# An S4 convolution beside a GEGLU FFN: products by half, a pairs contraction, port-spread rows, and four U spectra chunks in the phase buffers

## The chip, the cores and the metric

The kernel runs on one core of one Trainium2 chip. The engines named here are PE (matrix products; PEld is its weight load), DVE, ACT and POOL (elementwise work) and SP, which in this kernel only issues DMAs. The metric is the device time of one execution in microseconds, lower is better; the value before is the median of three runs.

## The reference

The function mixes two branches of one input u [1, 2048, 640] in bf16:

```python
x = A_u
g = _sigmoid((x * gate_w).sum(-1, keepdims=True))
a = _A_ref(x, ...)       # S4
b = _B_ref(x, ...)       # (gelu(x @ w_gate) * (x @ w_up)) @ w_down, 640 -> 1728 -> 640
return g * a + (1 - g) * b
```

```python
logdA = dt * A                      # [D=640, N=128], complex
dB = dt * Bc
P = jnp.exp(logdA[:, :, None] * l[None, None, :])
K = jnp.einsum("dn,dnl,dn->dl", Cc, P, dB).real
...
Yf = Uf * Kf[None, :, :, :]         # FFT of length 4096 of u and of K, both padded with zeros
y = irfft(Yf)[..., :L]  +  u * Dskip
```

So per channel a kernel K of 2048 steps is generated from 128 complex modes, and u is convolved with it causally by a transform of length 4096.

## The kernel before, in words

One tile `arena` [128 partitions, 211,968 bytes] holds everything; regions are addressed by byte offsets (`O_XT` to `O_UA`, L254 to L268) and shared by names that live at different times. `Plan` records each step with what it reads, writes and overlaps (L77 to L120); `emit` (L128) replays a written-out list `ORDER` (L27 to L74): each number gives step, engine and PSUM bank pair. The order of instructions on each engine is thus fixed, and every DMA is issued from the SP queue in that order. The time estimates that `add` takes (first argument) belong to the planner and change nothing on the chip unless `ORDER` does.

The work, in the order in which it mostly runs:

- **FFN.** The 2048 rows go in two groups. For each of 14 column tiles of 128 of the 1728 columns, `gate` (L500, 10 matmuls of 512 columns) with the gelu on ACT (L504), `up` (L520) with the product on DVE (L524). `downs` (L540): 8 steps per group, each 28 matmuls (L548), evicted scaled by 1 - g (L245 on ACT, L249 on DVE). Plain evictions from PSUM are L243 (ACT) and L247 (DVE).
- **K generation**, `kgen(q)`, for each half q of the channels (W = 320 each). cs1 and cs2 hold two grids of complex exponentials, with four channels side by side (`quads`): `exps1` (L599, 32 exponentials of 320 elements on ACT), `phases` (L580, L582, L584 on DVE, the sine L589 on ACT), `grid1` (L613 twice and L614 once per group of rows), `neg1` (L619), `exps2` (L627, then L631 on DVE), `grid2` (L637).
- **Contraction**, `contract` (L650): 80 groups of four channels, two matmuls each with 128 weight columns (32 rows x 4 channels) and 80 moving columns (20 x 4); of the 4 x 4 channel pairs in the result only the diagonal is wanted. Seven evictions to kst; `pick` (L661) selects the wanted quarter with the matrix sel, and dS (DRAM) takes the half of K by four writes (L678). The first row of K comes apart (L669, L672, L676).
- **U transform**: L719, evictions, 16 writes of dU (L724).
- **Gathers** (L744, L752): 18 DMAs per half read dS into Kl, 128 partitions x 16 phases x 320; partition ranges 0:16, 16:32, 32:64, 64:128 come from different rows of dS.
- **Stage A** (L780) transforms Kl; eight writes per half into columns W*h of one DRAM tensor dKA (L784).
- **Stage B** (L807): the second step of the transform, in eight chunks of 4 of the 32 DRAM row groups, loaded by `loadB` (L794), for U (from dU) and for K (from dKA, both halves of the channels, hence after both stage A). `swap` (L820): two DMAs inside the arena that give a copy of the U spectrum with neighbouring partitions exchanged.
- **`mix`**, one per chunk: stage B of K, two products on DVE over all 640 channels (L826, L827, 2560 elements each), the inverse step (L834, four PSUM steps), one write of dY (L840).
- **`finish`**: eight loads of dY (L847), each of which needs rows of all eight chunks, through a ring of four tiles; the last matmuls (L854), the additions of the FFN part (L859), and 16 output writes (L863).

All U chunks of the spectra lie in the region of cs1 and cs2, so none is loaded before the second contraction has read it.

Of the kernel before, what the change touches and what calls it, by code (L numbers as in the profile page):

```python
# [27 lines left out]
    336 1392 652 276 12 296 356 436 616 476 636 948 516 24 376 416 316 456 496 964 556 536 44 596 1468 576 224 676  # L28
    696 64 896 936 856 2740 1448 876 396 984 6316 796 1484 816 916 836 1408 716 736 1544 2981 2836 776 756 1064 1428
    2862 3076 1004 1024 1044 4383 2956 2768 1124 1084 1104 2888 10580 10604 3008 4404 2782 10636 1508 3020 2804 2856  # L30
    1568 1604 2903 3096 248 3044 88 3101 2976 4428 1664 2602 1148 6320 3196 6348 2624 2924 1168 6362 2656 3220 6436
    6388 1524 1188 6416 3128 3463 3316 3248 4444 3142 1584 3556 3488 1628 3261 3216 3164 1204 6440 1688 3336 6483
    3822 3284 6556 6464 6508 1644 3501 1228 3916 6536 3848 3340 3576 1244 1264 4183 1284 3368 3436 3524 1704 6562
    4208 4276 6600 3581 6676 6588 6628 6656 3703 1724 3608 3676 1304 3622 3728 3796 3940 3696 1324 3644 1348 4061
    4036 104 3968 6683 1364 4156 6722 1944 6796 4088 3860 6748 2004 6708 1748 6776 3981 3936 3884 3382 4056 1828
    1764 4004 1788 4223 3456 3404 1868 1804 4300 4296 1908 1844 4244 128 1924 3741 4376 1884 1968 144 6802 3816 6843
    6916 3764 6828 1984 6868 168 6896 4101 2064 2028 4176 4328 6922 2124 6963 7036 6988 6948 4344 2088 7016 184 4124
    2044 7043 208 7082 7068 4460 2184 7156 7108 2148 7136 2104 2164 2208 9464 7161 7203 4488 4742 7276 7188 2224
    7228 7256 9524 2480 4768 2321 2504 2443 2344 2242 2464 2360 2264 2281 2384 2403 2304 7322 2424 9728 7280 4661
    7396 7304 7344 9768 9744 7376 9808 2523 9784 2560 4684 4502 2588 2544 9848 9824 2716 2736 9408 2696 9864 2676  # L40
    7401 4524 7440 4703 7516 7424 9888 7464 8276 8296 8236 9448 9904 7496 8316 8436 8336 4542 4724 8456 8536 8576
    9388 8416 8356 8396 8496 8476 8556 7521 4564 7560 9428 8256 4583 7636 7584 8376 8516 7544 7616 9488 4622 4604
    9548 9584 7680 7641 4648 9504 4783 7756 7668 7708 7736 4902 4808 4876 9644 5021 9608 4996 9564 7760 5116 7803
    7876 7824 7788 9668 9924 5260 7856 5048 4823 5356 9984 4928 7921 4896 7948 4844 7882 7996 7908 4941 5288 9684
    7976 5142 5016 4964 10008 8003 5236 8040 9624 5061 8116 8068 5136 10104 8028 5300 9948 8096 5383 5376 5324 5168
    10044 8160 5476 5408 8122 8188 5503 5084 8148 8216 9964 5420 5528 5596 9704 10068 5742 10024 5496 5444 8621
    10128 5836 8583 10164 5180 8608 11176 11356 8648 5623 10144 5256 5768 8676 5204 5861 5716 5648 10084 10188 5782
    5956 5540 5804 5856 5888 11536 10204 8723 5616 8682 5564 8708 10221 8748 10262 8776 10244 10300 10284 10343
    10324 10381 10364 8822 10404 8780 8848 10423 8808 10462 8876 10444 11221 11260 10488 11244 11183 11288 11302
# [91 lines left out]
def kernel(  # L141
# [90 lines left out]
    def evac(n, p, dst, src, r=(), w=(), rank=3.0, act=True, dve=True, scale=None, **k):  # L232
        e = {}
        if act:
            e["ACT"] = an(n)
# [21 lines left out]
    O_WD = O_ZA + 10240  # L257
    O_W = O_WD + 17920
    O_TB = O_W + 7680
    O_WA = O_TB + 384  # L260
    O_A = O_WA + 8192
    O_CS1 = O_A + 11520
    O_CS2 = O_CS1 + 40960
# [302 lines left out]
    def quads(ap):  # L566
        return ap.rearrange("p (k j) -> p k j", j=4)
# [390 lines left out]
```

## Time and profile before

| | us |
|---|---|
| median of three runs (326.82, 326.91, 329.02) | 326.91 |
| profiled execution | 327.61 |
| its span | 325.8 |
| mean granted PE clock | 0.922 |

| engine | busy us (share of the span) |
|---|---|
| PE | 266.1 (82%) |
| DVE | 246.3 (76%) |
| ACT | 223.6 (69%) |
| POOL | 5.3 (2%) |

Times within the profile are counted from the start of the span. In the first 30 us PE is busy 20.18, DVE 19.82 and ACT 25.18 us. The 40 slices of the span (busy tenths; PEclk is the granted clock in tenths) show where no engine is full:

```profile
PE   0799999897796999979899987985998889993452
...
DVE  4687999999999963799996977254363899982464
ACT  4998997699995599998989576525471386671000
...
PEclk9989999999797999999999997999899799998555
DMA  6993344332321144433437659979366569934997
```

One slice is 8.1 us. The first contraction lies at 100.4 to 107.8 us (slices 13 and 14 from the left), the second at 182.3 to 194.3, the gathers of the second half after it, and the loads of dY in the last four slices. Mean durations of DMAs from issue to landing, as far as the change touches them: dU write (320 KB) 2.3 us, dU load (640 KB) 4.7, dKA write (320 KB) 4.2, dKA load (640 KB) 6.0, swap (320 KB) 4.3, dY write (640 KB) 6.1, dY load (640 KB) 5.6, output (160 KB) 4.7 (medians).

### The profile page before, as it was taken

How to read it: one execution, taken by the hardware profiler on the slowest of the kernel's cores; microseconds unless marked ns; L12 is line 12 of the kernel's file. 1: busy time of each engine (PE TensorE's matmuls, PEld its weight loads, DVE VectorE, ACT ScalarE, POOL GpSimd, SP SyncE). 2: the span in 40 equal slices, each digit the busy share in tenths (PEclk: the TensorE clock that was granted, in tenths of full speed). 3: DMA queues.
4: the chain of work that ended last, by engine and by line, in shares of the span. 5: the costliest groups of instructions: out<-in, count | busy, mean ns of one | idle time of the engine just before them, and what ended most of it. 6: DMA issues, size and time to landing. Idle time of an engine off the chain costs nothing.

```text
span 325.8 us, 5490 instructions
## 1 busy us (share of the span) xinstructions
PE 266.1 (82%) x2112; PEld 146.7 (45%) x2126; DVE 246.3 (76%) x332; ACT 223.6 (69%) x307; POOL 5.3 (2%) x18
## 2 busy tenths in 40 slices
PE   0799999897796999979899987985998889993452
PEld 0254444443366677534344743432465456551220
DVE  4687999999999963799996977254363899982464
ACT  4998997699995599998989576525471386671000
POOL 3000000000000000000000000000110000000000
PEclk9989999999797999999999997999899799998555
DMA  6993344332321144433437659979366569934997
GB/s 171 394 331 104 121 140 125 100 103 81 125 76 42 62 123 130 143 123 120 141 100 240 188 192 291 341 163 260 115 204 221 181 240 330 344 141 163 368 353 245
DMA packets 47519, 60.57 MB, mean 186 GB/s; under 512 B 4419, under 2 KB 41862, under 8 KB 47494
## 3 DMA queue, kind: packets, MB, share of 16 engines
q1 hardware_dynamic: 47494, 60.23, 57.3%
q8 instruction: 16, 0.26, 0.3%
q14 instruction: 9, 0.07, 0.1%
HBM read 35.80 MB, written 19.17 MB: 169 GB/s over the span
## 4 chain that ended last, share of the span: by engine, by line
PE 36%; ACT 22%; DVE 18%; DMA 15%; issue 5%; SPq 3%; DVEq 0%; ACTq 0%
PE ps L548 13%; PE ps L520 8%; PE ps L500 7%; ACT arena L243 6%; ACT arena L589 5%; DVE arena L247 5%; DMA dKA<-arena 4%; ACT arena L599 4%; DMA arena<-dY 3%; DMA arena<-dU 3%; ACT arena L504 3%; DMA arena<-dKA 2%; DVE arena L859 2%; PE ps L650 2%; PE ps L807 2%
## 5 line engine op out<-in xcount | busy, mean ns | idle before, releaser
L243 ACT CAST arena<-ps 128x640 bf16<-128x640 f32 x111 | 70.6, 702 | 38.1 <-PE ps L807 15.7
L500 PE MATMUL ps<-arena 128*128 128x512 bf16 x276 | 66.5, 392 | 13.0 <-DMA arena<-in_u_T_dram 9.2
L247 DVE CAST arena<-ps 128x640 bf16<-128x640 f32 (+2 forms) x67 | 56.2, 881 | 20.1 <-PE ps L807 10.4
L520 PE MATMUL ps<-arena 128*128 128x512 bf16 x250 | 63.1, 401 | 4.2 <-DVE arena L524 1.9
L548 PE MATMUL ps<-arena 128*128 128x320 bf16 x448 | 65.0, 305 | 1.0 <-DVE arena L247 0.5
L548 PEld LDWEIGHTS <-arena 128*128 128x128 bf16 x448 | 44.5, 100 | 20.6 <-issue 2.1
L500 PEld LDWEIGHTS <-arena 128*128 128x128 bf16 x280 | 28.0, 100 | 47.9 <-issue 14.1
L520 PEld LDWEIGHTS <-arena 128*128 128x128 bf16 x260 | 26.5, 103 | 37.2 <-issue 9.3
L589 ACT ACTIVATE arena<-arena 128x2560 bf16<-128x2560 int16 x18 | 41.6, 2334 | 0.4 <-DVE arena L637 0.3
L524 DVE TENSOR_TENSOR arena<-ps,arena 128x1024 bf16<-128x1024 f32 x26 | 31.6, 1218 | 13.1 <-PE ps L520 12.9
L504 ACT ACTIVATE arena<-ps 128x1024 bf16<-128x1024 f32 (+1 forms) x28 | 27.7, 1023 | 9.4 <-PE ps L500 9.2
L807 PE MATMUL ps<-arena 64*64 64x320 bf16 x256 | 16.9, 325 | 9.0 <-DMA arena<-dKA 2.8
L599 ACT ACTIVATE arena<-arena 128x320 bf16<-128x320 f32 x64 | 23.3, 455 | 1.0 <-DVE arena L451 1.0
L854 PE MATMUL ps<-arena 128*64 128x320 bf16 x64 | 10.2, 474 | 14.5 <-DMA arena<-dY 14.5
L859 DVE SCALAR_TENSOR_TENSOR arena<-ps,g_f,arena 128x640 bf16<-128x640 f32 x16 | 13.0, 878 | 11.9 <-PE ps L854 11.9
L249 DVE TENSOR_SCALAR arena<-ps,omg 128x640 bf16<-128x640 f32 x10 | 8.8, 883 | 14.9 <-PE ps L548 14.9
L627 ACT ACTIVATE arena<-arena 128x320 bf16<-128x320 f32 x40 | 14.8, 455 | 5.9 <-PE ps L650 5.9
L582 DVE SCALAR_TENSOR_TENSOR arena<-arena 128x320 int32<-128x320 f32 x40 | 16.9, 483 | 0.8 <-ACT arena L589 0.7
L650 PE MATMUL ps<-arena 128*128 128x80 bf16 x320 | 13.5, 212 | 3.8 <-DVE arena L637 2.8
L807 PEld LDWEIGHTS <-arena 64*64 64x64 bf16 x256 | 8.2, 107 | 17.7 <-issue 9.7
L650 PEld LDWEIGHTS <-arena 128*128 128x128 bf16 x320 | 13.3, 107 | 4.6 <-DVE arena L637 3.5
L780 PE MATMUL ps<-arena 128*128 128x320 bf16 x64 | 12.1, 308 | 4.1 <-DMA arena<-dS 2.3
(93 smaller groups left out, 240.8 us busy)
## 6 DMA issues: line engine op xcount, KB each, us to landing
arena<-in_w_gu_dram SPq DMA_DIRECT2D x52, 160.0 KB, 2.2
dU<-arena SPq DMA_DIRECT2D x16, 320.0 KB, 2.3
arena<-dU SPq DMA_DIRECT2D x8, 640.0 KB, 4.7
dKA<-arena SPq DMA_DIRECT2D x16, 320.0 KB, 4.2
arena<-arena SPq DMA_DIRECT2D x16, 320.0 KB, 4.3
arena<-dKA SPq DMA_DIRECT2D x8, 640.0 KB, 6.0
dY<-arena SPq DMA_DIRECT2D x8, 640.0 KB, 6.1
arena<-dY SPq DMA_DIRECT2D x8, 640.0 KB, 5.6
```

Source lines behind the costliest of these rows:

```text
L243: nc.scalar.copy(out=dst, in_=src(b))
L247: nc.vector.tensor_copy(out=dst, in_=src(b))
L500: nc.tensor.matmul(ps[:, k + j, :], lhsT=Wg[w][:, kt, :], rhs=xT[2 * grp + j][:, kt, :], start=(kt == 0), stop=(kt == NKT - 1))
L504: add({"ACT": an(1024)}, lambda s: nc.scalar.activation(out=HTall[0:p, :, f, :], in_=ps[0:p, plan.bank(g):plan.bank(g) + 2, :], func=ACT.G ...
L520: nc.tensor.matmul(ps[:, k + j, :], lhsT=Wu[w][:, kt, :], rhs=xT[2 * grp + j][:, kt, :], start=(kt == 0), stop=(kt == NKT - 1))
L524: add({"DVE": v1(1024)}, lambda s: nc.vector.tensor_tensor(out=HTall[:, :, f, :], in0=ps[:, plan.bank(u):plan.bank(u) + 2, :], in1=HTall[: ...
L548: nc.tensor.matmul(ps[:, k + h, 0:W], lhsT=HTq[q][:, f, 128 * j:128 * j + 128], rhs=Wd[f][:, W * h:W * h + W], start=(f == 0), stop=(f == ...
L589: ac(an(8 * W), lambda: nc.scalar.activation(out=t[:], in_=ph.bitcast(I16)[:, :, :, 0:32:2], func=ACT.Sin, scale=SIN_SCALE), r=[f"ph{k}"], ...
L599: nc.scalar.activation(out=cs1[:, 1, :, 4 * s:4 * s + 4], in_=quads(aT[:, ds]), func=ACT.Exp, scale=float(sg * (4 + 8 * i)))
L650: nc.tensor.matmul(ps[:, k + i // g, 80 * (i % g):80 * (i % g) + 80], lhsT=cs1[:, x, k0 + i, :], rhs=cs2[:, x, k0 + i, :], start=(x == 0), ...
L807: nc.tensor.matmul(ps[64 * y:64 * y + 64, k + x, 0:W], lhsT=TB[64 * x:64 * x + 64, 0, :], rhs=t[64 * x:64 * x + 64, 2 * a + y, HV[h]], sta ...
L859: add({"DVE": v1(D)}, lambda s, p=p, ph=ph, z=z: nc.vector.scalar_tensor_tensor(out=z, in0=ps[:, plan.bank(p):plan.bank(p) + 2, 0:W], scal ...
```

## The change

1. **Products by half.** dKA becomes two DRAM tensors, one per half, so that a write is contiguous over 2560 bytes and a load has 320 KB. `mix` is split into `product(h, ...)` and `inverse`; a half's products need that half's stage A alone, and an inverse step of half h that half's products alone. dY becomes three tensors of 64, 32 and 32 rows (chunks 0 to 3, 4 and 5, 6 and 7), read back by 24 loads into eight tiles that are all resident.
2. **Pairs contraction.** Two channels lie side by side instead of four; 160 pairs, as two column halves (y) of PE, 320 matmuls per half with 64 weight columns and 40 moving columns; four evictions instead of seven. `exps1` writes a row and its mirror with one instruction of 640 elements, by way of a negated copy aN of aT. The first row of K is computed before `kgen(0)`.
3. **Port-spread rows.** The partitions of the transform are permuted: rows 0:16, 16:32, 32:64, 64:128 of the gathers go to partitions with strides 8, 8, 4 and 2. The rows of u_nat are permuted in the host's layout, and the tables' row numbers follow (`rows`, `last_rows`, five more fields). A fourth matrix is added to TB; nothing uses it, as SWAPS lists all chunks.
4. **Four of the eight U chunks in the phase buffers.** Chunks 0 to 3 of the U spectra go to `O_CS1 + 79360` (that is `O_PH`, beyond cs1 and cs2), so that their loads and stage B can stand beside the second contraction in `ORDER`.

`ORDER` is another list. In it, two `downs` (56 matmuls, now L578) stand behind the last inverse, PE's second contraction is interleaved with stage A of half 0 and stage B of U, and half 0's products stand before stage A of half 1 or between it. Lines move: L500 to 530, L520 to 550, L548 to 578, L559 to 589, L589 to 619, L599 to 633, L613 to 647, L614 to 648, L631 to 665, L637 to 671, L650 to 697, L780 to 826, L784 to 830, L794 to 842, L807 to 853, L820 to 867, L826/827 to 874, L834 to 885, L840 to 893, L847 to 899, L854 to 908, L859 to 913, L863 to 917; the evictions L243, L247 to 245, 249.

```diff
-    cs1 = at(O_CS1, [128, 2, 80, 128], BF16, "cs1")
+    cs1 = at(O_CS1, [128, 2, 160, 64], BF16, "cs1")
-    cs2 = at(O_CS2, [128, 2, 80, 4 * NE], BF16, "cs2")
+    cs2 = at(O_CS2, [128, 2, 160, 2 * NE], BF16, "cs2")
-    trig = [at(O_TRIG + 5120 * k, [128, 2, 80, 16], BF16, f"trig{k}") for k in range(2)]
+    trig = [at(O_TRIG + 5120 * k, [128, 2, 160, 8], BF16, f"trig{k}") for k in range(2)]
-    phb = [at(O_PH + 10240 * k, [128, 2, 80, 16], I32, f"ph{k}") for k in range(2)]
+    phb = [at(O_PH + 10240 * k, [128, 2, 160, 8], I32, f"ph{k}") for k in range(2)]
...
-    dKA = dp.tile([128, 32, D], BF16, name="dKA")
-    dY = dp.tile([128, 32, D], BF16, name="dY")
+    dKA = [dp.tile([128, 32, W], BF16, name=f"dKA{h}") for h in range(2)]
+    dY = [dp.tile([n, 32, D], BF16, name=f"dY{q}") for q, n in enumerate((64, 32, 32))]
...
+    def rows():
+        v = nc.vector
+        m = sc8[:, 7:8]
+        v.tensor_scalar(out=m, in0=B2, scalar1=16.0, scalar2=P3, op0=ALU.mult, op1=ALU.add)
+        v.tensor_scalar(out=sc8[:, 8:9], in0=P2, scalar1=32.0, scalar2=None, op0=ALU.add)
+        select(v, m, B1, sc8[:, 8:9], m)
+        v.tensor_scalar(out=sc8[:, 8:9], in0=P1, scalar1=64.0, scalar2=None, op0=ALU.add)
+        select(v, m, B0, sc8[:, 8:9], m)
+        v.tensor_scalar(out=m, in0=m, scalar1=16.0, scalar2=None, op0=ALU.mult)
+        select(v, sc8[:, 11:12], B1, B2, B3)
+        select(v, sc8[:, 11:12], B0, B1, sc8[:, 11:12])
+        v.tensor_scalar(out=tM, in0=tM, scalar1=m, scalar2=None, op0=ALU.add)
...
+    def pairs(ap):
+        return ap.rearrange("p (k j) -> p k j", j=2)
...
     def exps1(q, i0, n):
-        ds = slice(W * q, W * q + W)
+        o, d = (O_A + 1280 * q) // 4, (O_NEG[q] - O_A - 1280 * q) // 4
+        v = arena[:].bitcast(FP32)
+        ab = v[:, o:o + 2 * d].rearrange("p (s c) -> p s c", s=2) if d > 0 else v[:, o + d:o - d].rearrange("p (s c) -> p s c", s=2)
+        ab = ab[:, :, 0:W].rearrange("p s (k j) -> p s k j", j=2)
+        c5 = cs1.rearrange("p q k (r j) -> p q r k j", j=2)
 
         def go():
             for i in range(i0, i0 + n):
-                for s, sg in ((15 - i, -1), (16 + i, 1)):
-                    nc.scalar.activation(out=cs1[:, 1, :, 4 * s:4 * s + 4], in_=quads(aT[:, ds]), func=ACT.Exp, scale=float(sg * (4 + 8 * i)))
-
-        ac(2 * n * an(W), go, r=["aT"], w=[("cs1", i0 // 4)], aset="exp", rank=RKQ[q] + P["e1"])
+                out = c5[:, 1, 15 - i:17 + i:2 * i + 1] if d < 0 else c5[:, 1, 16 + i:(14 - i if i < 15 else None):-2 * i - 1]
+                nc.scalar.activation(out=out, in_=ab, func=ACT.Exp, scale=float(4 + 8 * i))
+
+        ac(n * an(2 * W), go, r=["aT", f"aN{q}"], w=[("cs1", i0 // 4)], aset="exp", rank=RKQ[q] + P["e1"])
...
-        c5 = cs1.rearrange("p q k (r j) -> p q k r j", j=4)
-        t5 = t.rearrange("p q k (r j) -> p q k r j", j=4)
+        c5 = cs1.rearrange("p q k (r j) -> p q k r j", j=2)
+        t5 = t.rearrange("p q k (r j) -> p q k r j", j=2)
         lo = slice(15 - i0, 11 - i0 if i0 < 12 else None, -1)
-        hi = slice(64 + 4 * i0, 80 + 4 * i0)
+        hi = slice(32 + 2 * i0, 40 + 2 * i0)
                 nc.vector.tensor_tensor(out=c5[:, x, :, lo, :], in0=t5[:, x], in1=c5[:, 1, :, lo, :], op=ALU.mult)
-            nc.vector.tensor_tensor(out=cs1[:, :, :, hi], in0=t[:], in1=cs1[:, 1:2, :, hi].to_broadcast([128, 2, 80, 16]), op=ALU.mult)
+            nc.vector.tensor_tensor(out=cs1[:, :, :, hi], in0=t[:], in1=cs1[:, 1:2, :, hi].to_broadcast([128, 2, 160, 8]), op=ALU.mult)
...
-        c4 = cs2[:, 1, :, 4 * i0:4 * i0 + 16].rearrange("p k (e j) -> p k e j", j=4)
+        c4 = cs2[:, 1, :, 2 * i0:2 * i0 + 8].rearrange("p k (e j) -> p k e j", j=2)
-        ve(v2(1280), lambda: nc.vector.tensor_tensor(out=c4, in0=c4, in1=quads(magdt[:, ds])[:, :, None, :].to_broadcast([128, 80, 4, 4]),
+        ve(v2(1280), lambda: nc.vector.tensor_tensor(out=c4, in0=c4, in1=pairs(magdt[:, ds])[:, :, None, :].to_broadcast([128, 160, 4, 2]),
...
-        for k0 in range(0, 80, 12):
-            n = min(12, 80 - k0)
+        for k0 in range(0, 80, 24):
+            n = min(24, 80 - k0)
             g = n // 2
 
             def go(k, k0=k0, n=n, g=g):
                 for i in range(n):
                     for x in range(2):
-                        nc.tensor.matmul(ps[:, k + i // g, 80 * (i % g):80 * (i % g) + 80], lhsT=cs1[:, x, k0 + i, :],
-                                         rhs=cs2[:, x, k0 + i, :], start=(x == 0), stop=(x == 1))
-
-            p = pe(2 * n * 51, go, r=[("cs1", g2) for g2 in range(4)] + [("cs2", g2) for g2 in range(5)], rank=RC, cr=1.6)
-            evac(int(80 * n * 1.05), p, kst[:, :, k0:k0 + n].rearrange("p e (b g) -> p e b g", b=2),
-                 lambda k, g=g: ps[:, k:k + 2, 0:80 * g].rearrange("p b (g e) -> p e b g", e=80), w=[("kst", k0)], rank=RC)
+                        for y in range(2):
+                            nc.tensor.matmul(ps[64 * y:64 * y + 64, k + i // g, 40 * (i % g):40 * (i % g) + 40],
+                                             lhsT=cs1[:, x, 80 * y + k0 + i, :], rhs=cs2[:, x, 80 * y + k0 + i, :], start=(x == 0), stop=(x == 1))
+
+            p = pe(4 * n * 29, go, r=[("cs1", g2) for g2 in range(4)] + [("cs2", g2) for g2 in range(5)], rank=RC, cr=1.6)
+            evac(int(40 * n * 1.05), p, kst[:, :, k0:k0 + n].rearrange("p e (b g) -> p e b g", b=2),
+                 lambda k, g=g: ps[:, k:k + 2, 0:40 * g].rearrange("p b (g e) -> p e b g", e=40), w=[("kst", k0)], rank=RC)
...
+        def rows_of(m0):
+            return {0: slice(0, 128, 8), 16: slice(4, 128, 8), 32: slice(2, 128, 4), 64: slice(1, 128, 2)}[m0]
...
-            dst = Kl[m0:m1, phs, :]
+            dst = Kl[rows_of(m0), phs, :]
...
-            dma(160 * G, lambda t=t, g=g: nc.sync.dma_start(out=dKA[:, 2 * G * g:2 * G * (g + 1), W * h:W * h + W], in_=t),
-                r=[(nm, a) for a in range(G)], w=[("dKA", h, g)], rank=R, run=640)
+            dma(160 * G, lambda t=t, g=g: nc.sync.dma_start(out=dKA[h][:, 2 * G * g:2 * G * (g + 1), :], in_=t),
+                r=[(nm, a) for a in range(G)], w=[("dKA", h, g)], rank=R, run=2560)
...
+    def u_spec(u, us, bi, c, R):
+        b = loadB(dU[:], D, [("dU", ph) for ph in range(NPH)], bi, c, R)
+        ks = stageB(b, (0, 1), *u, R)
+        if c not in SWAPS:
+            return ks, stageB(b, (0, 1), *us, R, 3)
+        for q in range(2):
+            dma(320, lambda q=q: nc.sync.dma_start(out=us[0][q:128:2], in_=u[0][1 - q:128:2]), r=ks, w=[(us[1], q, h) for h in range(2)], rank=R, run=2560)
+        return ks, [(us[1], q, h) for q in range(2) for h in range(2)]
+
+    def product(h, u, us, kb, bi, c, UK, keys, R):
         (U, un_), (Us, sn), (t, tn) = u, us, kb
-        SK = [(sn, s) for s in range(2)]
-        ks = stageB(loadB(dKA[:], keys, bi, c, R), t, tn, R)
-        ve(v2(D * CS), lambda: nc.vector.tensor_tensor(out=U, in0=U, in1=t, op=ALU.mult), r=ks + SK, w=UK, rank=R - .1)
-        ve(v2(D * CS), lambda: nc.vector.tensor_tensor(out=Us, in0=Us, in1=t, op=ALU.mult), r=ks, w=SK, rank=R - .1)
+        ks = stageB(loadB(dKA[h][:], W, keys, bi, c, R), (0,), t, tn, R)
+        for x, kx in zip((U, Us), UK):
+            ve(v2(W * CS), lambda x=x: nc.vector.tensor_tensor(out=x[:, :, HV[h]], in0=x[:, :, HV[h]], in1=t, op=ALU.mult), r=ks,
+               w=[k for k in kx if k[2] == h], rank=R - .1)
+
+    def inverse(u, us, yb, c, UK, R):
...
+        q = max(0, c // 2 - 1)
+        s0 = CS * (c - (0, 4, 6)[q])
+        v = dY[q][:].rearrange("(s x) i w -> (x i) s w", x=4)
+        dma(640, lambda: nc.sync.dma_start(out=v[:, s0:s0 + CS, :], in_=t), r=[(tn, a, h) for a in range(CS // 2) for h in range(2)],
             w=[("dY", c)], rank=R - .2, run=1280)
-        return ("dY", c)
-
-    def finish(keys, rings, R):
-        for g in range(8):
-            t, nm = rings[g % len(rings)]
-            dma(640, lambda t=t, g=g: nc.sync.dma_start(out=t, in_=dY[:, 4 * g:4 * g + 4, :]), r=keys, w=[nm], rank=R, run=5120)
+
+    def finish(tiles, R):
+        for q, (p0, st, cs) in enumerate(((0, 2, (0, 1, 2, 3)), (1, 4, (4, 5)), (3, 4, (6, 7)))):
+            for g, (t, nm) in enumerate(tiles):
+                dma(640 // st, lambda t=t, g=g, q=q, p0=p0, st=st: nc.sync.dma_start(out=t[p0:128:st], in_=dY[q][:, 4 * g:4 * g + 4, :]),
+                    r=[("dY", c) for c in cs], w=[(nm, q)], rank=R + P["F0"] * (2 - q), run=5120)
...
-                p = pe(TF * 4 * mm(W), go, r=["WAT", nm], rank=R)
+                p = pe(TF * 4 * mm(W), go, r=["WAT"] + [(nm, q) for q in range(3)], rank=R)
...
-    bi = blocks(O_CS1 + 79360, 4, 5120, 3, "bi")
-    kb = blocks(O_CS1 + 94720, 4, 5120, 2, "kb")
-    U = blocks(O_CS1, 4, 5120, 8, "V")
-    Us = blocks(O_CS1 + 40960, 4, 5120, 4, "Vs")
-    Kl1 = at(O_CS1 + 61440, [128, NPH, W], BF16, "Kl1")
-    uk = [u_spec(U[c], bi, c, P["U1"]) for c in range(8)]
-    for c in range(4):
-        swap(U[c], Us[c], uk[c], P["U1"])
-    keys += stageA(1, Kl1, blocks(O_CS1 + 71680, 4, 2560, 3, "ar", W), 2, P["A1"])
-    kb += blocks(O_CS1 + 61440, 4, 5120, 2, "kc")
-    ys = []
+    U = blocks(O_CS1 + 79360, 4, 5120, 4, "V") + blocks(O_CS1, 4, 5120, 4, "Vb")
+    Us = (blocks(O_CS1 + 40960, 4, 5120, 4, "Vs") + blocks(O_A, 4, 5120, 2, "Vt") + blocks(O_W, 4, 5120, 1, "Vu") +
+          blocks(O_WA, 4, 5120, 1, "Vv"))
+    Kl1 = at(O_CS1 + 20480, [128, NPH, W], BF16, "Kl1")
+    b0 = blocks(O_A, 4, 5120, 2, "bi") + blocks(O_CS1 + 74240, 4, 5120, 1, "bj")
+    b1 = blocks(O_CS1 + 61440, 4, 5120, 1, "bk") + b0[2:]
+    kb = blocks(O_CS1 + 66560, 4, 2560, 3, "kb", W)
+    bh = blocks(O_CS1 + 61440, 4, 2560, 2, "bh", W) + blocks(O_CS1 + 74240, 4, 2560, 2, "bg", W)
+    uk = [u_spec(U[c], Us[c], b0, c, P["U0"]) for c in range(4)]
+    uk += [u_spec(U[c], Us[c], b1, c, P["U1"]) for c in range(4, 6)]
+    nk = [0]
+
+    def kbuf():
+        nk[0] += 1
+        return kb[nk[0] % 3]
+
+    for c in range(6):
+        product(0, U[c], Us[c], kbuf(), bh, c, uk[c], keys[0], P["C0"])
+    keys[1] = stageA(1, Kl1, blocks(O_CS1 + 30720, 4, 2560, 3, "ar", W), 2, P["A1"])
+    uk += [u_spec(U[c], Us[c], b1, c, P["U2"]) for c in range(6, 8)]
+    for c in range(6, 8):
+        product(0, U[c], Us[c], kbuf(), bh, c, uk[c], keys[0], P["C0"])
+    yb = blocks(O_CS1 + 20480, 4, 5120, 3, "yb")
     for c in range(8):
-        if c >= 4:
-            swap(U[c], Us[c % 4], uk[c], P["U1"])
-        ys.append(mix(U[c], Us[c % 4], kb[c % 4], bi, c, uk[c], keys, P["C1"]))
-    finish(ys, blocks(O_CS1, 4, 5120, 4, "as"), P["F1"])
+        product(1, U[c], Us[c], kbuf(), bh, c, uk[c], keys[1], P["C1"])
+        inverse(U[c], Us[c], yb[c % 3], c, uk[c], P["C1"])
+    finish(blocks(O_CS1 + 79360, 4, 5120, 4, "as") + blocks(O_CS1 + 40960, 4, 5120, 4, "at"), P["F1"])
...
+    p = _np.arange(128)
+    rows = _np.where(p % 2, 64 + p // 2, _np.where(p % 4, 32 + p // 4, _np.where(p % 8, 16 + p // 8, p // 8)))
```

## What I expected, before the result

> **What bounds the kernel now.** I read the totals first, then a table of engine busy time by stage, then the chain of waits, then the groups of instructions. All sums are made against the profiled execution: span 325.8 us, time 327.61 us, so 1.8 us lie around the span; the median of the three runs, 326.91, is 0.7 lower.
>
> Busy time of each engine in eight stretches (columns: length, PE, PEld, DVE, ACT, POOL, granted clock, DMA share, GB/s):
>
> ```profile
> 30.00:100.40 70.40, 61.63 (x297) 29.86 (x300) 67.86 (x90) 64.54 (x75) 0.00 (x0) 0.95 0.34 103
> 100.40:107.80 7.40, 7.40 (x161) 7.38 (x162) 6.85 (x11) 1.57 (x2) 0.00 (x0) 0.77 0.12 47
> 107.80:182.30 74.50, 69.27 (x402) 38.08 (x403) 61.17 (x81) 70.16 (x95) 0.00 (x0) 1.00 0.45 137
> 182.30:194.30 12.00, 10.68 (x225) 8.15 (x225) 10.91 (x12) 7.21 (x12) 0.00 (x0) 1.00 0.52 170
> 194.30:220.80 26.50, 21.82 (x147) 9.85 (x151) 13.39 (x15) 11.69 (x17) 0.00 (x0) 0.94 0.87 265
> 220.80:296.00 75.20, 64.88 (x683) 39.80 (x684) 52.25 (x53) 42.91 (x66) 2.09 (x2) 0.95 0.70 229
> 296.00:325.80 29.80, 10.25 (x67) 4.35 (x64) 14.01 (x18) 0.29 (x1) 0.00 (x0) 0.55 0.79 286
> ```
>
> Up to 182 us three engines are nearly full together: DVE 96% before the first contraction (100 us), ACT 94% after it. From 194 the DMAs are the fullest resource (0.87), then PE again (65 of 75). The last 29.8 us are a DMA chain with engines idle. That tail, piece by piece (start, length, what):
>
> ```profile
> 297.05 3.20 DMA dY<-arena
> 300.74 3.89 DMA arena<-dY
> 304.67 0.76 PE ps L854 x3
> 305.54 1.53 DVE arena L859 x2
> 307.13 4.85 DVE arena L859 x6
> 312.38 7.01 DMA arena<-dY
> 319.43 0.76 PE ps L854 x4
> ```
>
> Two DMA legs, eight additions, then a third leg of 7.01: four tiles are resident, and the other four load only when these are used. The groups I price from:
>
> ```profile
> L247 DVE CAST arena<-ps 128x640 bf16<-128x640 f32 (+2 forms) x67 | 56.2, 881 | 20.1 <-PE ps L807 10.4 <-PE ps L520 2.9 <-issue 2.4
> ...
> L650 PE MATMUL ps<-arena 128*128 128x80 bf16 x320 | 13.5, 212 | 3.8 <-DVE arena L637 2.8 <-DVE arena L247 0.5 <-ACT arena L504 0.5
> ...
> L613 DVE TENSOR_TENSOR arena<-arena 128x1280 bf16<-128x1280 bf16 x16 | 13.1, 819 | 0.3
> ...
> L859 DVE SCALAR_TENSOR_TENSOR arena<-ps,g_f,arena 128x640 bf16<-128x640 f32 x16 | 13.0, 878 | 11.9 <-PE ps L854 11.9
> ```
>
> **Part 1, the pairs contraction.** Before: 160 matmuls per half in 7.48 us, 47 ns each. After: 320, each with half the weight columns (64) and half the stream (40). Bounds for their spacing: 47 ns (nothing gained, 15.0 us) and 27 ns (L559, a 128-column weight load with one column of stream: 80 in 2.14 us; 8.6 us). Nearest row: L854, the same 128x64 weights: 8 in 1.28 us at clock 0.5, 160 ns with 320 columns, at two column tiles in parallel. Taking the stream away leaves about 28 to 29 ns, so I take 9.3 us: +1.8 per half on PE. On DVE seven evictions go to four (960, 960, 960, 320 elements, 1.15 us per 960): about -4 us per half. On ACT, 32 exponentials of 320 in 11.62 us become 16 of 640, at some 0.63 spacing (723 ns for a 640-element ACT operation, less overlap): 10.1, so -1.5 per half. Between the contractions all three engines' lists get shorter: DVE 61.5 to 61.1, ACT 57 to 55.3, PE 67.4 to 64.5, as counts times row durations in the new order.
>
> The doubt is access pattern: the values of one row now lie in runs of two bf16, one 4-byte word, where they were two words. The trace has no DVE row with single-word runs. Bounds: nothing, or loss of a doubled rate that the rows show: 1280 bf16 elements cost 0.82 (L613) as 640 fp32 elements do (L460, 822 ns), so without doubling they would cost what 2560 cost with it, 1.48 (L637): +0.67 us on L647 (16 instructions, was L613) and L665 (10, was L631). I take nothing, since the second source of L613 and its output already hop from run to run at 819 ns; the other end is a rival.
>
> [...]
>
> **Part 2, the port-spread rows.** About 27 added DVE operations at 0.14 to 0.25 us (the small operations of the first stage), 4 us. Cover: DVE is 19.82 of 30.0 us busy in the first 30; if the cover is gone, +4. The gathers' destinations now stride 2 to 8 partitions: 2.6 to 4.3 us to land now; I take -1 for the 18 of half 1 (0 to -4).
>
> Sum up to the second contraction (182.3): 0, bounds -3 (less work between contractions) and +6 (one more `downs` of 3.9 us stands ahead of the first contraction, and the small operations).
>
> **Part 3, four chunks in the phase buffers.** Four U loads, their stage B (L807, 32 matmuls a chunk, 8 in 0.47 us) and swaps move from after the contraction to beside it: PE alternates 96 L697, 8 to 32 L853, L826. From the start of the second contraction to stage A of half 1, PE's list sums to 35.3 us where it was 32.0; picks end at 14.9 where they ended at 12.0. +2.9, less 1 of the gathers: +2. What is passed on SP: the last two of four dS writes stand behind four swaps, each waiting for a chunk's four evictions; four dKA loads (320 KB) and a weight load stand before the first gather. Issue costs 0.31 to 0.6 us each, so some 3 us of queue; cover: those 26.5 us hold 21.82 of PE work, and the new order has more. Cover gone: rival B.
>
> **Part 4, products by half.** Spectra and products of half 0 need not wait for half 1, so they leave the stretch from stage A to the last inverse. PE's list there is 49.5 us against 60.9 (3.5 us of spectra earlier; two `downs`, 7.6 us, moved behind the last inverse). DVE's list is 56 in both: the 16 products of 2560 at 1.48 become 32 of 1280 at 0.82, +2.6 us over both halves. -11.4 on PE, +2 since DVE then is nearly the bound (56 of 75.2 - 11.4 = 63.8): -9.4. What is newly waited for: each inverse of a half needs only that half's products, so PE stands behind DVE as before, and behind PE's waiting inverse stand the next chunk's L853 and the `downs`; DVE's evictions wait for these in turn. The dKA writes of 2560-byte runs should land like dU writes (same 320 KB, 2.3 us) and not in 4.2: hidden in any case by the work between.
>
> **Part 5, the tail.** dY comes back by thirds: 64 rows (chunks 0 to 3) early, then 32 and 32, and all eight tiles are resident. Behind the last inverse: eviction 1.0, dY write 3.2 (its median is 6.1), load of the last 160 KB 2.4 (weights of that size: 2.2), first product 0.9, 16 additions at 0.80 (10 L859 in 8.01 us) = 12.9, last output 3.9: 24.3 against 29.8, -5.5. With the write at its median: -2.6. I take -5. The 56 L578 that now wait there fit into write and load (7.6 against 5.6 to 8.5); with that cover gone +2.
>
> Sum: 0 + 2 - 9.4 - 5 = -12.4. Profiled execution 327.61 - 12.4 = 315.2; less 0.7, **314.5 us** as median.
>
> **The rivals.** (A, slower) Single-word runs lose the doubled rate: 26 instructions, 0.67 each, +17.4 us on DVE, between 30 and 190 us, where DVE is over 90% busy in the phases and grids. Taken in full: 314.5 + 17.4 = 332. It eats the gain from 12.4/26 = 0.48 us per instruction if nothing covers it. For it: DVE was the fullest engine before 100 us. Against: the idle DVE time between contractions, 13 of 74.5 us, and the 4 us per half from evictions (in my sums already).
>
> (B) The SP queue: swaps and dKA loads before the gathers, at a DMA share of 0.87, put stage A off by 8 us (one landing of each kind, 4.3 swap and 3.9 load): 322.5; with the tail's write at 6.1 also, 325.
>
> (C) The column halves do not overlap: 47 ns per matmul, +5.7 per half: 326, no change.
>
> (D, better) PE's idle time in stage A to the last inverse falls from 14 (75.2 less 60.9) to 6, as DMA waits go with the smaller loads, and the gathers give 4 rather than 1: -8 - 3 = 304.
>
> **How the numbers follow.** Forecast 0.47, A 0.23, B 0.10, C 0.09, D 0.11. One per cent (3.3 us: 323.6 to 330.2) is about what a measurement of this kernel can tell from no change. Forecast, D and six tenths of B lie below: faster 0.64. C and the rest of B: 0.13. A: 0.23. The range goes from D, 304, to A's 332 (A with any further loss is left out, as is half of D).
>
> **What would show it.** L647 and L665 at 0.82 us (A wrong) or 1.48 (A right). 320 L697 spaced at 28 to 29 ns or 47 (C). The second contraction starting near 182. The first L826 of half 1 near 222 (B: 230), the last L885 near 288, a tail of 24 to 27 us with one DMA leg rather than three between the additions, and L908 waiting once for dY. The prediction is wrong if the phases and grids before 182 grow, whatever the rest gains.

## The result: 376.2 us where 314.5 was expected

| | before | after |
|---|---|---|
| median, us | 327.16 (326.82 to 329.02, 4 runs) | 376.2 (374.72 to 378.51, 4 runs) |
| ratio to before | 1 | 1.149, 95% interval [1.141, 1.157] |
| span of the profiled execution | 325.8 | 373.4 |
| mean granted PE clock | 0.922 | 0.859 |

Of the kernels e1 to e12 only e9 has runs that count as slow (over 1.5% above its fastest), two of six: its median over all is 314.4, and 313.5 without them.

The changed kernel is slower by 15%. Its engines have no more to do: DVE is busy 246.8 us (246.3 before), ACT 222.7 (223.6), PE 276.6 (266.1, at a mean granted clock of 0.859 against 0.922). The time is idle time, and it lies early. The busy tenths of the changed kernel, 40 slices of 9.3 us:

```profile
PE   0920089999859989956258999876985996999672
DVE  4960039999999975802159998731385858897185
ACT  2034399999999859814647898534455665454000
```

Two holes stand out, counting slices from 1: slices 3 to 5 (PE at 2, 0 and 0, DVE at 6, 0 and 0) and slices 18 to 21 (all three). Neither was there before. Four marks put numbers on them (first matmul of each contraction, start of the last inverse matmul, end of the span):

| | before | after | difference over the stretch |
|---|---|---|---|
| first contraction starts | 100.4 | 130.1 | +29.7 |
| second contraction starts | 182.3 | 233.0 | +21.0 |
| last inverse matmul | 295.7 | 343.4 | -3.0 |
| end | 325.8 | 373.4 | -0.1 |

The contractions' first matmuls, before and after (start, length, engine, line, instructions; in brackets how long the engine was idle before, and for what it waited):

```profile
100.36 7.48 PE L650 MATMUL ps<-arena 128*128 128x80 bf16 x160 [2.79 <-DVE arena L637]
182.32 4.46 PE L650 MATMUL ps<-arena 128*128 128x80 bf16 x120 [0.49 <-ACT arena L504]
```

```profile
130.06 1.70 PE L697 MATMUL ps<-arena 128*64 128x40 bf16 x96 [0.31 <-DVE arena L671]
233.00 1.70 PE L697 MATMUL ps<-arena 128*64 128x40 bf16 x96
```

The changed kernel's second contraction runs in pieces with other matmuls between them; another 96 of its matmuls start at 238.9.

The first hole. The changed kernel in order of time:

```profile
23.44 16.06 SPq L475 DMA_DIRECT2D arena<-in_B_w_down_dram  x11
26.95 2.65 ACT L633 ACTIVATE arena<-arena 128x640 bf16<-128x640 f32 x4 [5.93 <-DMA arena<-in_B_w_down_dram]
34.77 2.64 ACT L633 ACTIVATE arena<-arena 128x640 bf16<-128x640 f32 x4 [5.17 <-DMA arena<-in_B_w_down_dram]
...
43.04 2.65 ACT L633 ACTIVATE arena<-arena 128x640 bf16<-128x640 f32 x4 [5.62 <-DMA arena<-in_B_w_down_dram]
...
47.00 2.85 ACT L534 ACTIVATE arena<-ps 128x1024 bf16<-128x1024 f32 x3
48.07 0.59 PE L550 MATMUL ps<-arena 128*128 128x512 bf16 x1 [26.80 <-ACT arena L534]
```

The exponentials of half 0 (L633) wait three times for loads of `w_down`, which they neither read nor write. Those loads, on SP, are 16 us in issue because each batch waits in turn for the exponentials (us in all, times, longest):

```profile
SPq L475 <- ACT arena L633: 19.5, 3, 8.8
```

The first gelu (L534) stands behind the exponentials on ACT, and PE behind the gelu for 26.8 us.

The second hole, by the list of waits (who waited for what: us in all, times, longest):

```profile
ACT L619 <- DMA arena<-dS: 13.5, 2, 7.9
...
DVE arena L665 <- DMA arena<-dS: 10.3, 2, 6.8
DVE arena L610 <- DMA arena<-dS: 9.1, 1, 9.1
DVE arena L647 <- DMA arena<-dS: 8.0, 2, 5.0
```

The sine, the phases and the grids of half 1 wait for the gathers of half 0. They work in cs1, cs2, trig and ph; the gathers write `Kl0` in another region. So both holes are waits between instructions that share no byte. Such waits come from the framework that builds the program: it follows what each instruction touches and adds semaphores. The listing of the built program has them in plain sight, and it needs no chip (first exponential of half 0 in the changed kernel, then in the run e5 below; the names with DMAHW stand for DMAs, and in the trace L633 waits 16.7 us, in three times, for those of `w_down`):

```
L633 Activation arena<-arena 128x2x160x2 [waits DMAHW4_49,DMAHW1_49,DMAHW7_49,DVE_49,Pool_49]
L633 Activation arena<-arena 128x2x160x2 [waits DVE_49]
```

**Theory W**: the builder follows memory by coarse ranges. (1) The merged exponential reads aN and aT as one pattern with two pieces, and counts as a read of all between. In half 0 the pieces start at bytes 56,832 and 93,696 of the arena, 36 KB apart (the expectations of e1 and e5 say 100 KB, which is wrong), and the slots of w_down and the weights (59,392 to 84,992) lie between; in half 1 they are 7.5 KB apart within one region. (2) A DMA whose destination strides over partitions counts as a write of far more of the tile than it writes. **Rivals**: O, the new order is bad in itself; P, the strided DMAs are slow in themselves; F, the merged form of the exponential is.

### The profile page after: what moved, and what is told of

Its sections match the earlier page's. It is cut to its first block, busy times and chain, and to the rows that moved or that the text cites. A ratio compares the mean times of both kernels' runs of the same rounds, so it can differ in the third digit from the quotient of the medians.

```text
span 373.4 us, 6191 instructions
## 1 busy us (share of the span) xinstructions
PE 276.6 (74%) x2431; PEld 148.0 (40%) x2446; DVE 246.8 (66%) x373; ACT 222.7 (60%) x274; POOL 5.2 (1%) x17
## 4 chain that ended last, share of the span: by engine, by line
PE 32%; DVE 13%; DMA 13%; SPq 8%; ACT 7%; issue 3%; POOLq 0%; DVEq 0%; ACTq 0%
PE ps L530 11%; PE ps L550 8%; PE ps L578 5%; SPq L790 3%; DMA arena<-dS 3%; DMA arena<-arena 3%; PE ps L697 3%; DVE arena L249 2%; DMA dY<-arena 2%; ACT arena L245 2%; DVE arena L671 2%; SPq L899 2%; DVE arena L554 2%; ACT arena L661 2%; PE ps L853 2%
## 5 line engine op out<-in xcount | busy, mean ns | idle before, releaser
L530 PE MATMUL ps<-arena 128*128 128x512 bf16 x273 | 73.4, 426 | 30.7 <-DMA arena<-in_w_gu_dram 14.1
L245 ACT CAST arena<-ps 128x640 bf16<-128x640 f32 (+1 forms) x110 | 70.5, 695 | 38.4 <-PE ps L853 11.2
L550 PE MATMUL ps<-arena 128*128 128x512 bf16 x252 | 64.2, 403 | 29.4 <-ACT arena L534 27.0
L578 PE MATMUL ps<-arena 128*128 128x320 bf16 x448 | 65.4, 306 | 0.0
L249 DVE CAST arena<-ps 128x640 bf16<-128x640 f32 (+3 forms) x62 | 50.3, 848 | 20.1 <-PE ps L697 6.3
L554 DVE TENSOR_TENSOR arena<-ps,arena 128x1024 bf16<-128x1024 f32 x26 | 31.5, 1220 | 42.6 <-PE ps L550 42.6
L530 PEld LDWEIGHTS <-arena 128*128 128x128 bf16 x280 | 29.8, 107 | 70.9 <-issue 31.8
L578 PEld LDWEIGHTS <-arena 128*128 128x128 bf16 x448 | 43.9, 100 | 19.6 <-issue 1.1
L550 PEld LDWEIGHTS <-arena 128*128 128x128 bf16 x260 | 26.7, 103 | 62.6 <-issue 36.8
L633 ACT ACTIVATE arena<-arena 128x640 bf16<-128x640 f32 x32 | 21.2, 745 | 28.5 <-DMA arena<-in_B_w_down_dram 16.7
L534 ACT ACTIVATE arena<-ps 128x1024 bf16<-128x1024 f32 (+1 forms) x28 | 27.4, 1023 | 10.6 <-PE ps L530 10.5
L853 PE MATMUL ps<-arena 64*64 64x320 bf16 x256 | 18.9, 351 | 9.4 <-DMA arena<-dKA 2.7
L874 DVE TENSOR_TENSOR arena<-arena 128x1280 bf16<-128x1280 bf16 x32 | 24.5, 820 | 0.3
L762 PE MATMUL ps<-arena 128*128 128x320 bf16 x64 | 12.8, 315 | 8.0 <-ACT arena L534 5.6
L647 DVE TENSOR_TENSOR arena<-arena 128x1280 bf16<-128x1280 bf16 x16 | 13.1, 820 | 8.3 <-DMA arena<-dS 8.0
L661 ACT ACTIVATE arena<-arena 128x320 bf16<-128x320 f32 x40 | 16.5, 510 | 2.4 <-DMA arena<-dS 2.3
L612 DVE SCALAR_TENSOR_TENSOR arena<-arena 128x320 int32<-128x320 f32 x40 | 16.9, 486 | 0.0
L853 PEld LDWEIGHTS <-arena 64*64 64x64 bf16 x256 | 8.9, 114 | 20.2 <-issue 12.9
L665 DVE TENSOR_TENSOR arena<-arena 128x1280 bf16<-128x1280 bf16 x10 | 8.1, 821 | 11.6 <-DMA arena<-dS 10.3
```

The lines of the kernel that those rows point to most:

```text
L245: nc.scalar.copy(out=dst, in_=src(b))
L249: nc.vector.tensor_copy(out=dst, in_=src(b))
L530: nc.tensor.matmul(ps[:, k + j, :], lhsT=Wg[w][:, kt, :], rhs=xT[2 * grp + j][:, kt, :], start=(kt == 0), stop=(kt == NKT - 1))
L534: add({"ACT": an(1024) + 60}, lambda s: nc.scalar.activation(out=HTall[0:p, :, f, :], in_=ps[0:p, plan.bank(g):plan.bank(g) + 2, :], func= ...
L550: nc.tensor.matmul(ps[:, k + j, :], lhsT=Wu[w][:, kt, :], rhs=xT[2 * grp + j][:, kt, :], start=(kt == 0), stop=(kt == NKT - 1))
L554: add({"DVE": v1(1024)}, lambda s: nc.vector.tensor_tensor(out=HTall[:, :, f, :], in0=ps[:, plan.bank(u):plan.bank(u) + 2, :], in1=HTall[: ...
```

## The experiments

e1, e2, e3, e5, e6 and e11 were executed once each, the others four times or more.

**e1.** The exponentials as before, in the new layout:

```diff
-                out = c5[:, 1, 15 - i:17 + i:2 * i + 1] if d < 0 else ...
-                nc.scalar.activation(out=out, in_=ab, func=ACT.Exp, scale=float(4 + 8 * i))
+                for s, sg in ((15 - i, -1), (16 + i, 1)):
+                    nc.scalar.activation(out=cs1[:, 1, :, 2 * s:2 * s + 2], in_=pairs(aT[:, W * q:W * q + W]), ...)
```

> The changed kernel, with its 16 exponentials of 640 elements per half (which read aN and aT in one instruction, 100 KB apart in the arena for half 0) written again as 32 of 320 elements from aT alone. Theory W (the loss is waits that the builder adds because it follows memory by coarse ranges: the read from aN to aT counts as a read of all between them, the slots of w_down and of the gate and up weights included): the ping-pong of L633 and the w_down loads before 50 us goes, PE's wait of 26.8 us for the gelu falls below 5, first L697 near 105 instead of 130, time 376 - 25 = 351 (345 to 357). Rival O (the new order of the queues is bad in itself, for instance the w_down loads stand in front of the weights that PE needs): no more than 5 us, 371 or above.

Measured 352.9 us: 23 off, as W has it; O falls for this hole.

**e2.** In addition contiguous gathers:

```diff
-            return {0: slice(0, 128, 8), 16: slice(4, 128, 8), 32: slice(2, 128, 4), 64: slice(1, 128, 2)}[m0]
+            return {0: slice(0, 16), 16: slice(16, 32), 32: slice(32, 64), 64: slice(64, 128)}[m0]
```

> As the run before it, and the gathers write partitions 0:16, 16:32, 32:64, 64:128 again in place of strides 8, 8, 4, 2 (host rows and tables follow; the result is the same). Theory W (a write with a stride over partitions counts as a write of the whole arena, so exponentials, phases and grids of half 1 wait for the gathers of half 0 and the gathers for them): DVE's waits for arena<-dS (34 us in the sum of lines L610, L647, L665) go, another 20 to 30 us less than the run before it: 326 (320 to 333). Rival P (the strides themselves are what costs or helps in the DMAs, by their landing times): the waits of DVE stay, and the time changes by less than 5 us.

Measured 324.8: 28 more. In its list of waits no line of ACT or DVE waits for dS any longer.

**e3 and e4.** Tiles per region. In e3 nothing moves in memory against e1, and no instruction or DMA changes; only what the builder takes for one object does (e4 has contiguous gathers and dY loads besides):

```diff
-    arena = mp.tile([128, ARENA // 2], BF16, name="arena")
+    CUTS = [O_XT, O_HT, O_ZA, O_WD, O_W, O_TB, O_A, O_CS1, O_CS2, O_KST, O_PH, O_K2, O_UA, ARENA]
+    region = {a: mp.tile([128, (b - a) // 2], BF16, name=f"r{a}") for a, b in zip(CUTS, CUTS[1:])}
...
-        v = arena[:, off // 2:(off + size) // 2]
+        v = region[lo][:, (off - lo) // 2:(off + size - lo) // 2]
```

> As the first run (32 exponentials of 320), strided gathers, strided swaps and strided dY loads kept, but the arena is cut into 13 tiles at region borders, at the same offsets, so that the builder follows each region for itself. Same instructions, same order, same data movement. Theory W: as fast as the run with contiguous gathers or faster, since swaps and dY loads lose their added waits too: 320 (314 to 328), 25 us or more below the first run. Rival P: no change against the first run, 351 or 371.

> Region tiles, 32 exponentials of 320, contiguous gathers and contiguous dY loads: none of the added waits is left, and no port-spread either. Theory W with my prices: the forecast 314.5, plus 3 for the exponentials, plus 6 to 9 for the tail that I mis-sized (16 loads of dY at 0.6 us of SP issue each stand behind the last write): 322 (316 to 328), faster than before by 0 to 3%. The comparison with the run that keeps the strides gives the worth of the port spread by itself: within 3 us of each other if the spread is worth nothing, the strided one faster by 3 us or more if it is. Rival O: 360 or above.

e3: 314.9 us, with every stride kept, 38 below e1, from which it differs in the tiles alone. This separates W from P: the same strided DMAs are harmless once they cannot be taken for writes of other regions. It also ends O, as the order is that of the changed kernel. e4: 318.5 (316.75 to 318.91, ratio 0.970 [0.962, 0.977]). So the spread over partitions seems to be worth something after all; e10 says where.

Of the 38 us, contiguous gathers alone gave 28 (e2). The other 10 lie between the second contraction and the last inverse matmul: 111.0 us in e2, 100.5 in e3, 100.3 in e4. In e2 the strided swaps (L861) wait 5.9 us for evictions on DVE and 3.8 us for the sine of WAT in another region, in e3 2.9 us for PE and 0.7 us for DVE. That the 10 us are the swaps' is argued from these lists; no run changes the swaps alone.

**e5.** The merged exponentials kept, but reading adjacent bytes:

```diff
+            if q == 0:
+                nc.vector.tensor_copy(out=aNT[:, 1], in_=aT[:, 0:W])
...
+        ab = (aNT if q == 0 else v).rearrange("p s (k j) -> p s k j", j=2)
```

> The changed kernel in one arena, strided gathers kept, and the 16 exponentials of 640 elements kept too; only for half 0 the values of aT are copied beside aN (one more DVE copy of 320 elements), so that each instruction reads 2560 adjacent bytes instead of two pieces 100 KB apart. Theory W (the reach of the read is what costs): as the run with 32 exponentials of 320, 352 (347 to 356), L633 waits for no load of w_down. Rival F (the form with 640 elements and mirrored rows is what costs, or its place in the order): 371 or above.

Measured 350.8. The form of the instruction is innocent (F falls); its reach was the cost.

**e6.** The kernel before, with strided gathers and nothing else:

```diff
-            dst = Kl[0:16, ph:ph + 7, :]
+            dst = Kl[0:128:8, ph:ph + 7, :]
```

> The kernel before, with nothing changed but the partitions that its gathers write: strides 8, 8, 4 and 2 in place of 0:16 to 64:128 (the tables stay, so the rows of K meet other rows' factors and the output differs). Theory W (a write with a stride over partitions counts as a write of the whole arena): exponentials and phases of half 1 wait for the gathers of half 0, some 20 to 30 us: 350 (343 to 358). Rival P (the cost of the strides in the changed kernel came from its order): within 3 us of 327.

Measured 351.5, 24 us more than before, by an edit that moves no instruction. In its list of waits the exponentials (L599), L631 and the sine (L589) of half 1 now wait for the gathers of half 0; the kernel before has no such line on ACT or DVE:

```profile
ACT arena L599 <- DMA arena<-dS: 16.1, 3, 5.7
DVE arena L631 <- DMA arena<-dS: 5.7, 1, 5.7
ACT L589 <- DMA arena<-dS: 4.3, 1, 4.3
```

**e7 and e9.** Region tiles, merged exponentials with adjacent reads (in e9, half 1 reads two pieces 7.5 KB apart within one region), and 12 loads of dY instead of 24:

```diff
-                dma(640 // st, lambda t=t, g=g, ...: nc.sync.dma_start(out=t[p0:128:st], in_=dY[q][:, 4 * g:4 * g + 4, :]),
+                    if (q, g ^ 1) in done:
+                        g0 = g & ~1
+                        nc.sync.dma_start(out=wide[g0 // 2][p0:128:st], in_=dY[q][:, 4 * g0:4 * g0 + 8, :])
```

> Region tiles, strided gathers, exponentials of 640 with adjacent reads in both halves, and the 24 loads of dY issued as 12, each for two neighbouring tiles (same bytes). Tests my tail: in the run with region tiles 16 loads at 0.6 us of SP issue lie behind the last dY writes, and the last seven of them on the chain (3.8 us). If issue bounds the tail, 2 to 4 us come off: 311.5 (309 to 314). If the dY write of 9 us bounds it, less than 1 us: 314. ACT's 3 us of saved exponentials bring nothing where ACT does not set the end.

> As the run with region tiles, adjacent reads and 12 loads of dY, with the negated values of half 1 kept in a place of their own (before, they lay over the first half of aT). Same instructions: 314 (312 to 316), ratio to before 0.955 to 0.970. It is the candidate that is faster than both kernels.

In e7 the negated values of half 1 overwrite the first half of aT while half 0 still reads it, so K of half 0 differs; its order and its times are those of e9. e7: 314.1 (313.28 to 314.58); e9: 314.4 (312.51 to 317.35), ratio 0.957 [0.954, 0.960]. If issue bounded the tail I expected 311.5; it was the other branch, 314: half the issues brought nothing that stands out of e3's one time. The tail, from the last inverse matmul to the end, is 31.5 us in e7 and 30.9 in e9, 30.4 in e3. The merged exponentials did bring something at their place: the second contraction starts at 179.5 and 179.7, in e3 at 182.2. The chain of e7 shows what its loads wait for, the last dY write, which takes 9.2 us:

```profile
277.36 9.18 DMA dY<-r
...
287.06 3.49 DMA r<-dY
```

**e8.** The control: region tiles (eight) for the kernel before.

> The kernel before with its arena cut into region tiles (eight; cs1 to the end is one), nothing else. Control: how much of the gain of the region tiles belongs to the change. Theory W: before has strided writes in its swaps alone, late and in the one region that stays whole, so 0 to 3 us: 325.5 (323 to 328). If region tiles are worth as much to it as to the changed kernel (60 us, or 10 beyond the exponentials and the gathers), the gain is not the change's.

Measured 326.0 (325.1 to 327.16, 10 runs), ratio 0.998 [0.994, 1.002]: nothing. The kernel before had no such waits to lose.

**e10.** e3 with contiguous dY loads (`t[p0:p0 + 128 // st]` for `t[p0:128:st]`, tables to match).

> Region tiles, strided gathers, but the 24 loads of dY into partitions 0:64, 64:96, 96:128. With both strided the run gave 314.9, with both contiguous 318.5. If the spread of the dY loads is what is worth the 3.6 us (their 160 KB land in 5.5 us contiguous, 2.8 strided; dY writes beside them in 7.5 against 5.7): 318 (316.5 to 320). If it is the spread of the gathers: 315 (313.5 to 316.5).

Measured 321.2 (320.76 to 322.61), ratio 0.980 [0.977, 0.984]. The spread of the dY loads is worth some 6 us: the tail is 36.8 us in e10, 35.6 in e4 and 30.4 in e3. Issue to landing, median us by size, in e10 and then in e3:

```profile
dY<-r SPq DMA_DIRECT2D x8, 640.0 KB, 7.7
r<-dY SPq DMA_DIRECT2D x8, 320.0 KB, 6.6
r<-dY SPq DMA_DIRECT2D x16, 160.0 KB, 5.3
```

```profile
dY<-r SPq DMA_DIRECT2D x8, 640.0 KB, 5.7
r<-dY SPq DMA_DIRECT2D x8, 320.0 KB, 5.2
r<-dY SPq DMA_DIRECT2D x16, 160.0 KB, 2.8
```

The loads of 160 KB into 32 partitions in a row take 5.3 us, the same bytes into every fourth partition 2.8, and the writes beside them take 7.7 us against 5.7. By what the spread does this no run shows. With both contiguous (e4) the time was 2.6 us lower than with the gathers alone strided (e10); those two ran on different chips, so whether the strided gathers cost something stays open. The -1 that I credited to them does not show: from the second contraction to the last inverse matmul, where the gathers of half 1 lie, e4 takes 100.3 us and e10 99.7.

**e11.** The changed kernel with contiguous gathers alone.

> The changed kernel with contiguous gathers alone; the wide read of the exponentials stays. Completes the two by two: 376 with both, 351 to 353 without the wide read, 325 without both. Theory W, two independent groups of waits at different places (before 50 us and 150 to 200 us): 348 (343 to 353). If the waits cover one another: 365 or above.

Measured 352.7. The two by two in one arena: 376 with both, 353 without the wide read, 353 without the strided gathers, 325 without both. Either cause alone adds 28 us to the 325, and 23 to 24 to the other; both together add 51. They are two separate causes at different places, and about 5 us of them cover each other.

**e12.** e9 with every second gather of half 1 on POOL's queue:

```diff
-            dma(..., lambda: nc.sync.dma_start(out=dst, in_=src), ...)
+            dma(..., lambda: (nc.gpsimd if h == 1 and i % 2 else nc.sync).dma_start(out=dst, in_=src), ...)
```

> As the candidate, with every second gather of half 1 issued from POOL's queue instead of SP's. In the run with region tiles the 18 gathers of half 1 stand on the chain with 0.6 us of issue each, 212 to 225 us. If issue sets the start of stage A: 2 to 4 us less, 311 (309 to 313). If PE's own list (21.98 us busy of 25.8 in that stretch) or the landing sets it: within 1 us of the candidate. If POOL's queue takes more than 1.3 us for a gather: slower, 316 or above.

Measured 310.1 (309.65 to 313.81), ratio 0.950 [0.945, 0.955], on the chip on which e9 gave 313.5: 3.4 us less. POOL issues its nine in 5.3 us, SP the other nine in 6.3, though POOL's land in 4.9 to 5.8 us (medians by size), where SP's in e9 take 2.2 to 3.6. In order of time:

```profile
206.06 0.66 POOL L798 DMA_DIRECT2D r<-dS  x1 [202.25 <-ACT r L539]
209.69 0.50 POOL L798 DMA_DIRECT2D r<-dS  x1 [2.97 <-DMA r<-in_w_gu_dram]
210.20 0.55 POOL L806 DMA_DIRECT2D r<-dS  x1
210.75 3.59 POOL L798 DMA_DIRECT2D r<-dS  x6
```

Issue on SP does hold up stage A of half 1, though not its start: the first matmul stands at 222 us in both, the last four start at 236.3 here and at 239.3 in e9, with no wait of PE for a gather left. This is the fastest version found, faster than both kernels.

## Why the prediction failed, step by step

**The step that failed** is the one that is missing. Every wait in my sums came from the kernel's own account of reads and writes, and I put the sum up to the second contraction at 0, bounds -3 and +6. Measured: +50.7 (29.7 + 21.0), with the second contraction at 233.0 where I had named 182 as the sign; in e3, without the waits, it starts at 182.2. Parts 1 and 2 each carried a wait that the account does not know: the merged exponential (I credited it with -1.5 us per half on ACT) cost 23 to 28, the gathers' strides (I credited -1) cost 24 to 28. From there to the last inverse matmul the changed kernel gained 3.0 where I forecast 7.4; e3 gains 12.9, so some 10 us more of waits stand in that stretch. None of the rivals was this one. Rival A named the right half of the kernel for a wrong reason: L647 and L665 kept their time within 5 ns.

```profile
L647 DVE TENSOR_TENSOR arena<-arena 128x1280 bf16<-128x1280 bf16 x16 | 13.1, 820 | 8.3 <-DMA arena<-dS 8.0
...
L665 DVE TENSOR_TENSOR arena<-arena 128x1280 bf16<-128x1280 bf16 x10 | 8.1, 821 | 11.6 <-DMA arena<-dS 10.3 <-ACT arena L661 1.3
```

820 and 821 ns against 819 and 816: neither is slower by anything near the 670 ns of rival A. In L647 the single words follow each other downward in runs of four; L665 hops with one source only, which repeats one word four times. Of other forms these two lines tell nothing. The same lines hold the true cause, in the idle time after the bar.

**The terms, once the waits are gone.** e3 is the changed order without them (and with 32 exponentials in place of 16), so the other steps can be read there: e3 ends at 314.9 against a forecast of 314.5, but two of its four terms were wrong, in opposite directions. Its second contraction starts here:

```profile
182.22 1.70 PE L697 MATMUL ps<-r,r 128*64 128x40 bf16 x96
```

Busy time by stretch of e3 (columns as in the prediction): the first 30 us, from the second contraction to stage A of half 1, from there to the last inverse matmul, and the tail.

```profile
0.00:30.00 30.00, 18.35 (x142) 8.53 (x142) 23.09 (x79) 24.70 (x43) 3.13 (x15) 1.00 0.83 269
...
182.20:223.00 40.80, 34.09 (x537) 18.39 (x534) 22.42 (x26) 20.51 (x28) 0.00 (x0) 0.92 0.79 256
223.00:283.00 60.00, 52.49 (x603) 31.67 (x604) 50.27 (x66) 36.61 (x56) 2.09 (x2) 0.94 0.81 264
283.00:313.10 30.10, 16.48 (x124) 10.12 (x120) 15.99 (x20) 0.52 (x1) 0.00 (x0) 0.76 0.83 251
```

- Up to the second contraction: -0.1 (182.2 against 182.3), forecast 0. DVE is busy 23.09 us in the first 30, 19.82 before: the small operations that I counted as covered add 3.3, and the first contraction starts 2.2 later. From the first to the second contraction it is then 79.6 us, 82.0 before.
- From there to stage A of half 1: 40.8 us (223.0 less 182.2) against 38.5, +2.3, forecast +2.
- From there to the last inverse matmul (282.7 in e3, 295.7 before): 59.7 against 74.9, -15.2; forecast -9.4. This is where the change pays: products of half 0 and four chunks of U done early, and two `downs` moved away. I kept too much idle time for PE: 16.3 us (65.8 less a list of 49.5), where it was 7.5 (60.0 less 52.49); rival D had it at -8 more.
- The tail: 30.4 against 30.1, forecast -5. The third DMA leg is gone as expected, but the two that are left grew: the last write took 9.0 us where I took 3.2, and 16 loads are 10.04 us in issue on SP, of which I counted none. Nine of these stand on the chain behind the write (288.2 to 293.1), yet e7, with half as many loads, has a tail no shorter: their number alone does not set it.

```profile
278.59 5.93 SPq L893 DMA_DIRECT2D dY<-r  x3
288.22 10.04 SPq L899 DMA_DIRECT2D r<-dY  x16
```

- The contraction: I took 28 to 29 ns per matmul between 27 and 47, an estimate from L854's 160 ns, of which no row gives the stream's share alone. Measured, in the chain of the changed kernel:

```profile
130.06 1.70 PE ps L697 x96
...
132.66 2.68 PE ps L697 x159
```

2.68 us by 159 is 16.9 ns, under my lower bound, so rival C falls. The contraction gains nothing by it: from its first matmul to the end of its last, the first contraction takes 8.6 us (130.06 to 138.67) where it took 7.5. In between PE has 1.4 us of other matmuls (L762) and is idle for 1.35 us without a releaser that the profile shows; what holds it there is open.

- Rival B, the SP queue, would have put the start of stage A of half 1 at 230; it is at 223.0. But issue is not free there either: e12 got 3.4 us out of it.

The sum 0 + 2 - 9.4 - 5 = -12.4 was met by -0.1 + 2.3 - 15.2 + 0.3 = -12.7. The first two terms were right. The other two were wrong by 5.8 and 5.3 us in opposite directions, so that e3 comes out at the forecast is luck.

## What to carry to other kernels

Before pricing a change to a kernel that holds its buffers in one object, list the waits of the built program and look for semaphores that the data do not need; a strided destination or a pattern that spans two far places can tie together parts that share no byte, and here 51 us hung on it (376 against 325), with DVE and ACT no busier than before. If layouts must stride, give each region that lives for itself an object of its own: same bytes, same order, and here 353 became 315 (e1 and e3). And count a DMA's issue, not only its landing: nine loads of 160 KB on one queue were 4.9 us on the chain here (e3). Whether fewer of them on that queue shorten the time, a run has to say: for the gathers it was 3.4 us (e12), for the dY loads nothing (e7).

## What the runs showed of the hardware

Two column tiles of PE started a 64-column weight load with a 40-column stream every 16.9 ns (159 in 2.68 us, changed kernel), below the 27 ns of the 128-column load with one column (80 in 2.14 us, before). Reading DRAM into 32 neighbouring partitions took 5.3 us for 160 KB (e10), into every fourth one 2.8 (e3). POOL's queue issued nine gathers in 5.3 us and SP's nine in 6.3 (e12), and POOL's landed in 4.9 to 5.8 us. On single 4-byte words in falling order DVE took 820 ns for 1280 bf16 (L647 of the changed kernel), on pairs of them 819 (L613, before).
